# Rest blocks, value weights and key pieces in another order: a two-layer attention kernel on one core

## The chip, the cores and the metric

The kernel runs on one core of a Trainium2 chip. The metric is the device time of one execution in microseconds (us), lower is better. Before the change three runs gave a median of 2765.46 us (2764.1 to 2766.71).

The core's engines work beside each other, each through its own instructions in program order: TensorE (PE, matrix products; PEld are its weight loads), VectorE (DVE), ScalarE (ACT), GpSimd (POOL) and SyncE (SP, which here only issues DMAs).

## The reference

Two attention layers A and B read the same input and are mixed by a gate. Sequence S = 2048, width D = 640, 32 heads of width 20:

```
x = A_x
g = sigmoid((x * gate_w).sum(-1, keepdims=True))
# for z in A, B, with that layer's wqkv and wo:
qkv = (x @ wqkv) split into q, k, v of 32 heads x 20
p   = softmax(q @ k^T * 20 ** -0.5)
o_z = (p @ v) put together to 2048 x 640, @ wo
out = g * o_A + (1 - g) * o_B
```

## The kernel before, in words

**Numbers.** Products of projections run in half precision in two parts: each operand is scaled by a power of two and split into a high and a low part (hi, lo), and three products hi*hi, hi*lo, lo*hi are summed. A projection of 512 positions is thus 15 matmuls (5 slices of the width, three products each). The probabilities and values are multiplied in single precision (line 690).

**Main loop.** Heads are worked in groups of four: 8 groups a layer, 16 in all (numbered from 0, so "the third group" is g = 2 and "the seventh" is g = 6). For each group there are 4 blocks of 512 queries, and for each block 8 steps of two key tiles of 128: 512 steps G (lines 1175 to 1213). One step holds eight score products on TensorE (line 672), each followed by an exponential on ACT (line 675), the value products of the step before (line 690), and eight products for maxima of a later block (line 614), which VectorE reduces (line 625). Softmax maxima are found up to 15 steps ahead. For some heads the maximum over two key chunks a and b is found from the product with the key difference a - b: ACT takes its positive part (line 618), and VectorE adds the product with b and reduces (line 622). The differences of keys are in tiles KD; GpSimd makes them (`key_differences`, lines 494 to 502: five operations), and DMAs spread them into their rows (`spread_differences`).

**Order inside a step.** A step follows one of three handwritten strings STEP (lines 54 to 56): e is a score, m a maximum, V a value product and X a piece of projection work. There is no X in the first string, one in the second, two in the third. Line 1187 picks it: none if no work in the list `fill` may start yet, two if the work is behind its due times, else one. `slot` (line 1125) takes the entry with the earliest due step and runs one of its pieces at each X, until its pieces are used up.

**Pieces.** `project_a` projects the keys and part of the queries of a group, four chunks of 512 positions. APARTS says in how many pieces each chunk of a group is cut, CUTS at which columns (5: 104 or 96 wide; 6: 88 or 80; 4: 128). Every piece is 15 matmuls (line 407) and one move out of the accumulator by ACT (line 434). The keys of g = 2 may start at step 15, due 24 to 36; those of g = 6 at step 136, due 152 to 164. The values' pieces (`project_v`, two for each pair of position tiles) and later the output products stand in the same list.

**Before the main loop** (lines 867 to 1033): input and weights are loaded, scaled and split; x is transposed on TensorE; the keys of group 0 are projected by chunks `a_chunk(0)` to `a_chunk(3)`, each followed by DMAs that spread the rows over the partitions. These DMAs alternate between the SP queue and the POOL queue (`both`, line 945), so a DMA on POOL stands in line with GpSimd's computing. The part of the queries that did not fit beside the keys ("rest") is projected by `r_chunk(0)` to `r_chunk(3)`, one for each block of 512 queries. Then:

- The maxima of the first two query blocks are found (lines 1022 to 1028), two halves for each block. A half has eight units, each of four maxima: two of key differences and two of keys. The first half reads KD[0] (chunks 0 and 1), the second KD[1] (chunks 2 and 3). The heads go in the order (1, 0), so rows 64 to 123 are read first.
- After each unit `go_on` hands TensorE as many matmuls of the series `rest` as that unit's share of the estimate `whole` allows. `rest` holds `r_chunk(1)`, the split of the values' weights (`values_begin`), `r_chunk(2)`, `r_chunk(3)`, the scales for the next group, and all values of the first two groups.
- `split_now` (line 343) splits the values' weights: one copy on ACT (line 344), a scaling (345) and a subtraction (346) on GpSimd, once for 5 x 160 columns and once for the 5 of the gate.

Of the kernel before, what the change touches and what calls it, by code (L numbers as in the profile page):

```python
# [14 lines left out]
OP = mybir.AluOpType  # L15
# [9 lines left out]
NT = S // P  # L25
NC = D // P
# [9 lines left out]
XE = 7  # L36
QKS = 2.0 ** -12
CUTS = {3: (0, 176, 344, 512), 4: (0, 128, 256, 384, 512), 5: (0, 104, 208, 312, 416, 512), 6: (0, 88, 176, 264, 344, 432, 512)}
APARTS = {2: 5, 3: 4, 4: 4, 5: 4, 6: 6}
RPARTS = {1: 4}  # L40
OB = 3
STORED, LOADED = 10, 18
# [19 lines left out]
T_SCORE, T_MODE, T_VALUES, T_READY = 0.217, 0.1, 0.85, 0.39  # L62
# [9 lines left out]
def kernel(  # L72
# [10 lines left out]
    nc = tc.nc  # L83
# [29 lines left out]
    inv_x = consts.tile([P, 1], F32, name="inv_x")  # L113
    inv_g = consts.tile([P, 1], F32, name="inv_g")
# [110 lines left out]
    def set_qk(i, r, inv):  # L225
        nc.vector.tensor_copy(r_qk[i], r)
        e = esc[i]
        nc.vector.tensor_tensor(e, inv[:, 0:1], inv_x, op=OP.mult)
        nc.vector.tensor_scalar(e, e, inv[:, 1:2], float(DH ** -0.5 / QKS ** 2), op0=OP.mult, op1=OP.mult)
        nc.vector.tensor_tensor(e, e, inv_x, op=OP.mult)  # L230

    def set_v(gg, r, inv):
        nc.vector.tensor_copy(r_v[gg], r)

        f = gg % (NG // 2) * 160
        while f < (gg % (NG // 2) + 1) * 160:
            p0 = f % P
            n = min(P - p0, (gg % (NG // 2) + 1) * 160 - f, (P, 32, 64, 32)[p0 // 32])
            nc.vector.tensor_copy(wrow[gg // (NG // 2)][p0:p0 + n, f // P:f // P + 1], inv[p0:p0 + n])
            f += n  # L240
# [102 lines left out]
    def split_now(t, r, hi, lo):  # L343
        nc.scalar.activation(hi, t, AF.Copy, scale=r)
        nc.gpsimd.tensor_scalar(t, t, r, None, op0=OP.mult)
        nc.gpsimd.tensor_tensor(lo, t, hi, op=OP.subtract)
# [7 lines left out]
    def block_tiles(kind):  # L354
        n = 2 if kind == "a" else 1
        return (wts.tile([P, NC, P], F16, name="wbh", tag=f"wh{kind}", bufs=n),
                wts.tile([P, NC, P], F16, name="wbl", tag=f"wl{kind}", bufs=n))
# [58 lines left out]
    def project_chunk(w, hi, lo, ch, parts=None):  # L416

        wh, wl = w
        def pairs(n):
            if now[0] < 0:  # L420
                return ([(wh[:, c, :], b[:, c, n]) for c in range(NC) for b in (xh, xl)]
                        + [(wl[:, c, :], xh[:, c, n]) for c in range(NC)])
            return [(a[:, c, :], b[:, c, n]) for c in range(NC) for a, b in ((wh, xh), (wh, xl), (wl, xh))]

        t0 = ch * QB
        if now[0] >= 0:
            f = work.tile([P, QB], F32, name="fs")
            for k in range(len(parts) - 1):
                if k:
                    yield  # L430
                m = slice(parts[k], parts[k + 1])
                i, pt = take()
                yield from mms(i, pt[:, m], pairs(slice(t0 + m.start, t0 + m.stop)), (m.stop - m.start) / QB)
                nc.scalar.activation(f[:, m], pt[:, m], AF.Copy, scale=QKS)  # L434
                give(i, spend("act", 0.25, clock["done"]))
            nc.gpsimd.tensor_copy(hi, f)  # L436
            nc.gpsimd.tensor_tensor(lo, f, hi, op=OP.subtract)
        else:
            i, pt = take()
            yield from mms(i, pt, pairs(slice(t0, t0 + QB)), 1)  # L440
            give(i, spend("dve", T_MAX, spend("act", T_EXP, clock["done"])))
            nc.scalar.activation(hi, pt, AF.Copy, scale=QKS)
            nc.vector.scalar_tensor_tensor(lo, pt, QKS, hi, op0=OP.mult, op1=OP.subtract)

    def run(gen):
        for _ in gen:
            pass
# [10 lines left out]
    def spread(g, hl, t0, n, q=(0, 1), k=(0, 1), queues=repeat(nc.sync)):  # L458


        cols = slice(t0, t0 + n)
        r0 = 32 * (g % 4)
        qt = QT[g % 2]
        for j in range(2):
            base = 64 * j
            for pair in k:
                f = slice((2 * pair + j) * DH, (2 * pair + j + 1) * DH)
                yield from rows(KT[g % 2][:, pair, cols], base, 0, hl[f], DH, True, queues)
            if 0 in q:
                f = slice(GF + j * DH, GF + (j + 1) * DH)  # L470
                yield from rows(qt[:, 0, cols], base, 0, hl[f], DH, False, queues)
            if 1 in q:
                if j == 0:
                    yield from rows(qt[:, 1, cols], base, 0, hl[GF + 40:P], 8, False, queues)
                f = slice(r0 + 12 * j, r0 + 12 + 20 * j)
                yield from rows(qt[:, 1, cols], base, 8 * (1 - j), rk[g // 4][f, :, cols], 12 + 8 * j, False, queues)
# [6 lines left out]
    def project_r(i, ch):  # L483
        n = slice(ch * QB, (ch + 1) * QB)
        yield from project_chunk(blk["r", i], rk[i][:, 0, n], rk[i][:, 1, n], ch, CUTS[RPARTS.get(i, 3)])
        r_done.add((i, ch))
# [7 lines left out]
    def key_differences(g, hl, f, dd):  # L494

        n = GF
        differences[g] = dd
        nc.gpsimd.tensor_tensor(f[:n], hl[:n, 0, :QB], hl[:n, 0, QB:], op=OP.subtract)
        nc.gpsimd.tensor_tensor(f[:n], f[:n], hl[:n, 1, :QB], op=OP.add)
        nc.gpsimd.tensor_tensor(f[:n], f[:n], hl[:n, 1, QB:], op=OP.subtract)  # L500
        nc.gpsimd.tensor_copy(dd[:n, 0], f[:n])
        nc.gpsimd.tensor_tensor(dd[:n, 1], f[:n], dd[:n, 0], op=OP.subtract)

    def spread_differences(g, queues=repeat(nc.sync), to=None):
        dd = differences.pop(g)
        for j in range(2 if g == 0 else 1):
            for pair in range(2):
                f = slice((2 * pair + j) * DH, (2 * pair + j + 1) * DH)
                yield from rows((KD[g % 2] if to is None else to)[:, pair], 64 * j, 0, dd[f], DH, True, queues)

    def project_a(g, ch):
# [3 lines left out]
        n = slice((ch % 2) * QB, (ch % 2 + 1) * QB)  # L515
        yield from project_chunk(blk["a", g], hl[:, 0, n], hl[:, 1, n], ch, CUTS[APARTS.get(g, 3)])
        if ch == 1:
# [17 lines left out]
    def v_tiles(gg):  # L535
        blk["v", gg] = (wts.tile([P, NC, 161], F16, name="wvh", tag="wvh", bufs=1),
                        wts.tile([P, NC, 161], F16, name="wvl", tag="wvl", bufs=1))
        return blk["v", gg]
# [333 lines left out]
    wv = start.tile([P, NC, 161], F32, name="wv")  # L872
# [50 lines left out]
    hi, lo = blk["a", 0] = block_tiles("a")  # L923
# [8 lines left out]
    hi, lo = blk["r", 0] = block_tiles("r")  # L932
# [23 lines left out]
    def r_chunk(ch, pairs):  # L956
        yield from project_r(0, ch)
        n = slice((ch % 2) * QB, (ch % 2 + 1) * QB)
        run(spread(0, halves[ch // 2][:, :, n], ch * QB, QB, q=pairs, k=(), queues=both))
        spread_done.add((0, ch))  # L960
# [8 lines left out]
    def series(*gens):  # L969
        for gen in gens:  # L970
            yield from gen

    def differences_of(half, to):
        key_differences(0, halves[half], start.tile([P, QB], F32, name="fd"), start.tile([P, 2, QB], F16, name="dd0"))
        run(spread_differences(0, both, to))
# [16 lines left out]
    next(chain)  # L992
    run(chain)
    rv, invv = of_v
    differences_of(1, KD[1])

    def values_begin():
        hi, lo = v_tiles(0)
        split_now(wv[:, :, :160], rv[:, 0:1], hi[:, :, :160], lo[:, :, :160])
        split_now(wv[:, :, 160:161], rv[:, 1:2], hi[:, :, 160:161], lo[:, :, 160:161])  # L1000
        nc.vector.tensor_scalar(inv_g, invv[:, 1:2], inv_x, -1.0, op0=OP.mult, op1=OP.mult)
        yield True

    def next_group():
        set_qk(0, r[:, 0:2], inv[:, 0:2])
        set_v(0, rv[:, 0:1], invv[:, 0:1])
        split_next()
        yield True

    rest = series(r_chunk(1, (0, 1)), values_begin(), r_chunk(2, (0, 1)), r_chunk(3, (0, 1)), next_group(),  # L1010
                  *(project_v(0, j) for j in range(0, NT, 2)))

    halves_done = [0]
    streamed[0] = 0.0
    whole = (3 * 3 * NC + NT * 3 * NC * 0.33) * T_SCORE

    def go_on(share):

# [36 lines left out]
    for g in range(2 * NG):  # L1055
        b = g * step
        n = g + 1
        if n < 2 * NG:
            parts = APARTS.get(n, 3)
            fill += [((-8, 15)[g] if g < 2 else b + AFROM, b + ADUE + ADUES * ch if g else 4 + 3 * ch, parts, project_a(n, ch))  # L1060
# [188 lines left out]
```

## Time and profile before

| What | Value |
|---|---|
| Median of three runs | 2765.46 us |
| The profiled execution | 2765.39 us, span 2763.6 us |
| PE | 2725.5 us, 99% of the span |
| ACT | 2525.4 us, 91% |
| DVE | 2441.0 us, 88% |
| POOL | 671.5 us, 24% |
| DMA | 125.60 MB, mean 45 GB/s |

The profile is of one execution. A row of a timeline gives start, duration (both us), engine, line, operation, tiles (out<-in), shapes and count; in square brackets stands how long the engine was idle before, and what ended it. A row of the chain of work gives start, duration, and what was on the chain. A row of a table by stage gives the stretch, its length, then for each engine its busy time and, in brackets, its instructions; then the granted TensorE clock (1.00 is full), the DMA share and GB/s. Where such a table is restricted to one line of the code, it counts only that line's instructions. Matmuls are pipelined, so their durations overlap; starts are better read than durations.

### The profile page before, as it was taken

Reading aid. Unit: us, or ns where it says so; the run is one execution under the profiler, and the core shown is the slowest. Engines: PE = TensorE matmul, PEld = TensorE weight load, DVE = VectorE, ACT = ScalarE, POOL = GpSimd, SP = SyncE. Lnnn points to the kernel's source line nnn. Section 1 sums busy time; section 2 is a strip of 40 time slices with the busy share of each in tenths; the row PEclk is TensorE's granted clock in tenths of the full one; section 3 lists DMA queues with packets and bytes.
Section 4 is the critical chain, followed back from the end, with each engine's and each line's share of the span. In section 5 each row is a group of like instructions: output and inputs, shape, how many; then the busy total and the mean of one; then the engine's idle time right before and its main releaser. Section 6 shows DMA issues by size and latency. Waiting matters only on the chain.

```text
span 2763.6 us, 62604 instructions
## 1 busy us (share of the span) xinstructions
PE 2725.5 (99%) x23453; PEld 938.0 (34%) x23453; DVE 2441.0 (88%) x4780; ACT 2525.4 (91%) x5140; POOL 671.5 (24%) x914
## 2 busy tenths in 40 slices
PE   7999999999999999999999999999999999999998
PEld 3433333333333332333333333333333333333222
DVE  7789999999999889888888998989988898999982
ACT  4999999999999999999999899999999999999997
POOL 6322223222123422311222111222342202100111
PEclk8999999999999999999999999999999999999999
DMA  4021102010120212102012230221201112122112
GB/s 142 17 57 26 31 11 47 8 31 16 25 55 20 60 35 56 41 9 61 20 41 66 60 84 26 60 56 48 65 16 42 30 50 63 32 77 64 47 47 76
DMA packets 176433, 125.60 MB, mean 45 GB/s; under 512 B 105216, under 2 KB 145976, under 8 KB 176128
## 3 DMA queue, kind: packets, MB, share of 16 engines
q1 hardware_dynamic: 173584, 119.99, 17.0%
q8 instruction: 183, 3.00, 0.5%
q0 software_dynamic: 1600, 0.96, 0.2%
q14 instruction: 122, 1.00, 0.1%
q10 hardware_dynamic: 944, 0.66, 0.1%
HBM read 55.53 MB, written 31.86 MB: 32 GB/s over the span
## 4 chain that ended last, share of the span: by engine, by line
PE 93%; DVE 4%; ACT 1%; DMA 1%; issue 0%; POOL 0%; SPq 0%; POOLq 0%; DVEq 0%; ACTq 0%
PE acc L690 35%; PE bank L407 20%; PE bank L614 20%; PE bank L672 18%; DVE mpart L625 2%; ACT pt L675 1%; DMA ws<-in_A_wqkv_dram 0%; DVE rl L622 0%; PE bank L854 0%; DVE ot L777 0%; DMA xs<-in_A_x_dram 0%; PE bank L900 0%; ACT rl L618 0%; DVE wmax L258 0%; DMA kd<-dd 0%
## 5 line engine op out<-in xcount | busy, mean ns | idle before, releaser
L675 ACT ACTIVATE pt<-bank 128x512 f32<-128x512 f32 x4096 | 2173.2, 615 | 147.9 <-PE bank L672 105.3
L625 DVE TENSOR_REDUCE mpart<-bank 128x1 f32<-128x512 f32 x2944 | 1842.4, 681 | 220.7 <-PE bank L614 117.4
L690 PE MATMUL acc<-pt,v 128*21 128x512 f32 x8192 | 1081.7, 600 | 0.7 <-DVE ot L777 0.6
L672 PE MATMUL bank<-qt,kt 64*128 64x512 f16 x4096 | 1039.1, 380 | 4.7 <-DVE mpart L625 2.7
L614 PE MATMUL bank<-kt,qt 60*128 60x512 f16 x3520 | 1010.6, 381 | 3.6 <-DVE mpart L625 1.0
L614 PEld LDWEIGHTS <-qt 60*128 60x128 f16 x4096 | 237.9, 94 | 906.8 <-issue 846.1
L622 DVE CUSTOM_DVE_ANT_0 rl<-bank,rl 128x512 f32<-128x512 f32 x576 | 386.7, 677 | 13.3 <-ACT rl L618 8.6
L618 ACT ACTIVATE rl<-bank 128x512 f32<-128x512 f32 x576 | 339.6, 600 | 11.9 <-PE bank L614 11.3
L407 PE MATMUL bank<-xx,wbh 128*128 128x168 f16 (+7 forms) x2600 | 291.4, 234 | 1.5 <-DVE wbh L926 1.0
L672 PEld LDWEIGHTS <-kt 64*128 64x128 f16 x4096 | 229.2, 94 | 178.8 <-issue 69.9
L690 PEld LDWEIGHTS acc<-pt,v 128*21 128x21 f32 x8192 | 143.0, 99 | 426.2 <-issue 421.9
L407 PE MATMUL bank<-xx,wbl 128*128 128x168 f16 (+7 forms) x1300 | 259.9, 232 | 0.0
L785 POOL TENSOR_TENSOR ot<-ot,sq 128x512 f32<-128x512 f32 x63 | 66.0, 1047 | 736.7 <-DVE sq L782 718.1
L407 PEld LDWEIGHTS <-wbh 128*128 128x128 f16 x2600 | 196.5, 98 | 118.4 <-issue 112.7
L614 PE MATMUL bank<-kd,qt 60*128 60x512 f16 x576 | 204.3, 380 | 2.3 <-DMA kd<-dd 2.2
L436 POOL CAST cq<-fs 128x512 f16<-128x512 f32 x60 | 36.6, 610 | 500.8 <-ACT fs L434 500.8
L407 PE MATMUL bank<-woh,o_in 128*128 128x320 f16 (+3 forms) x700 | 157.7, 290 | 0.0
L407 PE MATMUL bank<-wvh,xx 128*128 128x160 f16 (+1 forms) x1280 | 156.0, 234 | 0.0
L407 PEld LDWEIGHTS <-xx 128*128 128x128 f16 x1920 | 131.3, 97 | 56.1 <-issue 53.8
L407 PE MATMUL bank<-wvl,xx 128*128 128x160 f16 (+1 forms) x640 | 137.6, 232 | 0.0
L407 PEld LDWEIGHTS <-wbl 128*128 128x128 f16 x1300 | 127.4, 98 | 4.4 <-issue 1.3
L407 PEld LDWEIGHTS <-o_in 128*128 128x128 f16 (+1 forms) x1050 | 87.3, 97 | 90.7 <-issue 68.5
(140 smaller groups left out, 1251.8 us busy)
## 6 DMA issues: line engine op xcount, KB each, us to landing
y_scr<-y_out SPq DMA_DIRECT2D x48, 320.0 KB
y_out<-y_scr SPq DMA_DIRECT2D x32, 320.0 KB
kt<-cq SPq DMA_DIRECT2D x120, 80.0 KB
o_scr<-on SPq DMA_DIRECT2D x240, 40.0 KB
o_in<-o_scr SPq DMA_DIRECT2D x64, 96.0 KB
kt<-cq SPq DMA_DIRECT2D x136, 40.0 KB
wstage<-in_B_wqkv_dram SPq DMA_DIRECT2D x13, 400.0 KB
xs<-in_A_x_dram SPq DMA_DIRECT2D x8, 640.0 KB
```

What stands on the lines that cost most here:

```text
L407: nc.tensor.matmul(out_ap, a, b, start=(k == 0), stop=(k == len(pairs) - 1))
L436: nc.gpsimd.tensor_copy(hi, f)
L614: nc.tensor.matmul(pt, QT[g % 2][r, pair, q0:q0 + P], k, start=True, stop=True)
L618: nc.scalar.activation(relus[u, j], pt, AF.Relu)
L622: nc.vector.tensor_tensor_reduce(rl, pt, rl, 1.0, LOW, OP.add, OP.max, m)
L625: nc.vector.tensor_reduce(m, pt, axis=AX.X, op=OP.max)
L672: nc.tensor.matmul(et, KT[g % 2][r, pair, kt * P:(kt + 1) * P], QT[g % 2][r, pair, qb * QB:(qb + 1) * QB], start=True, stop=True)
L675: nc.scalar.activation(pt, et, AF.Exp, scale=factor(g // 4))
L690: nc.tensor.matmul(acc[32 * h:32 * h + VW, :], V[(g // 2) % 2][:, kt, (g % 2) * GH + h, :], ptiles.pop((G, kk, h)), start=(kt == 0), stop= ...
L785: nc.gpsimd.tensor_tensor(t3, t3, sq.unsqueeze(2).to_broadcast([P, 16, 32]), op=OP.mult)
```

## The change

Three things move. The values' weights are split right after their scales are known, ahead of the second key differences (KD[1]); before, this stood in `rest` behind `r_chunk(1)`. `r_chunk(1)` runs ahead of the first maxima, and is no longer in `rest`; `whole` is reduced by its share. And the keys of g = 2 and g = 6 are cut into four pieces a chunk instead of five and six.

```diff
-APARTS = {2: 5, 3: 4, 4: 4, 5: 4, 6: 6}
+APARTS = {2: 4, 3: 4, 4: 4, 5: 4, 6: 4}
...
     run(chain)
     rv, invv = of_v
+    hi, lo = v_tiles(0)
+    split_now(wv[:, :, :160], rv[:, 0:1], hi[:, :, :160], lo[:, :, :160])
+    split_now(wv[:, :, 160:161], rv[:, 1:2], hi[:, :, 160:161], lo[:, :, 160:161])
+    nc.vector.tensor_scalar(inv_g, invv[:, 1:2], inv_x, -1.0, op0=OP.mult, op1=OP.mult)
     differences_of(1, KD[1])
-
-    def values_begin():
-        hi, lo = v_tiles(0)
-        split_now(wv[:, :, :160], rv[:, 0:1], hi[:, :, :160], lo[:, :, :160])
-        split_now(wv[:, :, 160:161], rv[:, 1:2], hi[:, :, 160:161], lo[:, :, 160:161])
-        nc.vector.tensor_scalar(inv_g, invv[:, 1:2], inv_x, -1.0, op0=OP.mult, op1=OP.mult)
-        yield True
+    run(r_chunk(1, (0, 1)))
...
-    rest = series(r_chunk(1, (0, 1)), values_begin(), r_chunk(2, (0, 1)), r_chunk(3, (0, 1)), next_group(),
+    rest = series(r_chunk(2, (0, 1)), r_chunk(3, (0, 1)), next_group(),
                   *(project_v(0, j) for j in range(0, NT, 2)))
...
-    whole = (3 * 3 * NC + NT * 3 * NC * 0.33) * T_SCORE
+    whole = (2 * 3 * NC + NT * 3 * NC * 0.33) * T_SCORE
```

## The prediction

> **What bounds the kernel now.** I read the page's chain of work that ended last, then the same chain cut to the first 160 us, then engine timelines there, and last a table by stage for the main loop.
>
> ```profile
> span 2763.6 us, 62604 instructions
> ...
> PE 93%; DVE 4%; ACT 1%; DMA 1%; issue 0%; POOL 0%; SPq 0%; POOLq 0%; DVEq 0%; ACTq 0%
> PE acc L690 35%; PE bank L407 20%; PE bank L614 20%; PE bank L672 18%; DVE mpart L625 2%; ACT pt L675 1%; DMA ws<-in_A_wqkv_dram 0%; DVE rl L622 0%; PE bank L854 0%; DVE ot L777 0%; DMA xs<-in_A_x_dram 0%; PE bank L900 0%; ACT rl L618 0%; DVE wmax L258 0%; DMA kd<-dd 0%
> ```
>
> TensorE carries 93% of the chain. So an edit counts if it removes TensorE work or TensorE idle time, or if a step becomes so short that another engine ends it.
>
> Two stages change. The first is the stage before the main loop, up to the first scores (line 672):
>
> ```profile
> 49.45 2.27 DMA kd<-dd
> 51.86 0.71 PE bank L614 x4
> ...
> 67.81 0.54 PE bank L614 x4
> 68.35 0.97 PE bank L407 x4
> ...
> 72.93 0.95 PE bank L407 x12
> ...
> 104.86 0.58 PE bank L672 x4
> ```
>
> At 51.86 the first maxima wait for a DMA of key differences. Afterwards TensorE alternates between four maxima (a "quartet", 0.54) and a piece of the "rest" (0.97 for four 512-wide matmuls, 0.95 for twelve of the values' 161-wide ones, switching included). The stage ends at 104.86.
>
> The second is the main loop: 512 steps of eight exponentials on ACT. A step has room for one piece X of projection work. Below, each window starts and ends at a step's first exponential, found by counting eight L675 instructions a step. The first table counts them; the second gives every engine (PE, PEld, DVE, ACT, POOL).
>
> ```profile
> 188.01:288.32 100.31, 86.55 (x161) 1.00 0.10 21
> 793.78:913.83 120.05, 104.61 (x192) 1.00 0.13 32
> 303.82:343.65 39.83, 33.98 (x65) 1.00 0.09 20
> 425.33:434.74 9.41, 8.16 (x16) 1.00 0.05 10
> ```
>
> ```profile
> 188.01:288.32 100.31, 100.02 (x944) 32.91 (x941) 95.00 (x192) 94.61 (x204) 23.57 (x35) 1.00 0.10 21
> 793.78:913.83 120.05, 119.22 (x1130) 37.73 (x1129) 114.36 (x224) 111.97 (x241) 41.79 (x46) 1.00 0.13 32
> 303.82:343.65 39.83, 39.83 (x378) 14.03 (x376) 36.57 (x69) 38.18 (x81) 5.46 (x9) 1.00 0.09 20
> 425.33:434.74 9.41, 9.23 (x68) 2.12 (x70) 9.13 (x19) 8.91 (x19) 6.67 (x6) 1.00 0.05 10
> ```
>
> From the top: the third group's keys in fifths, 20 steps, 100.31/20 = 5.02 a step; the seventh group's in sixths, 24 steps, 5.00 a step; keys in quarters, 8 steps, 4.98 a step; two steps with no X, 4.71 each. (A stray exponential at a window's edge makes 161 and 65.) In the third row TensorE has no gap. In the fourth VectorE is busy 9.13 of 9.41: without X it is VectorE that nearly ends the step.
>
> **Edit 1: rest block 1 and the values' split move ahead.** TensorE and GpSimd are in-order queues here, so I follow both.
>
> ```profile
> 42.60 2.32 PE L407 MATMUL bank<-xx,wbh 128*128 128x512 f16 x10
> 44.76 0.59 PE L407 MATMUL bank<-xx,wbl 128*128 128x512 f16 x2
> ...
> 49.32 0.38 PE L195 MATMUL bank<-dg,ones 2*128 2x4 f32 x2
> 51.86 0.50 PE L614 MATMUL bank<-kd,qt 60*128 60x512 f16 x2 [2.16 <-DMA kd<-dd]
> ...
> 66.38 0.39 PE L614 MATMUL bank<-kd,qt 60*128 60x512 f16 x2
> ```
>
> ```profile
> 47.76 1.99 POOL L455 DMA_DIRECT2D kd<-dd  x4
> ...
> 55.25 1.17 POOL L498 TENSOR_TENSOR fd<-cq 80x512 f32<-80x512 f16 x1
> ...
> 60.74 1.99 POOL L455 DMA_DIRECT2D kd<-dd  x4
> ...
> 65.27 2.30 POOL L345 TENSOR_SCALAR wv<-wv,both 128x800 f32<-128x800 f32 x1
> ...
> 69.96 1.06 POOL L455 DMA_DIRECT2D qt<-cq  x2
> ```
>
> *What it fills.* Ten matmuls start 42.60 to 44.76, 0.216 each. Block 1 is 15 of them, 3.24 us. Its operands are there at 49.70, where the scales' product (L195) ends, so it fills the idle 2.16 us and puts the first maxima at 52.94 instead of 51.86. Four maxima plus the switch to and fro are 0.54 + 0.97 - 4 x 0.216 = 0.65.
>
> *What it delays.* GpSimd is in unbroken work from 47.76 to 69.96: DMA issues, second differences (55.25 to 60.74, 5.49), issues of KD[1] and of block 1's queries, then the values' split (65.27 to 69.96, 4.69). The change puts the split first. It starts at 55.25, the differences at 59.94, and they end at 65.43. Behind them, in the POOL and SP queues alike, stand KD[1]'s DMAs and block 1's query rows. KD[0] needed 51.86 - 47.76 = 4.10 from the end of its differences to the matmul that reads it (j = 1 is read first, issued third on SP). So KD[1] can be read at 65.43 + 4.10 = **69.53**.
>
> *Who waits.* The first matmul on KD[1] is the first of the second half of block 0, the ninth quartet, at 66.38 before. `go_on` hands out rest by shares of `whole`: after 8 of 32 quartets a quarter, (45 + 79.2)/4 = 31.05 before, so 32 matmuls; (30 + 79.2)/4 = 27.3 now, so 28. Hence TensorE would come to it at 52.94 + 28 x 0.216 + 8 x 0.65 = 64.2. It waits about 5.3 us, and everything behind it in TensorE's queue waits too. The idle time is not removed; it moves and grows.
>
> *What comes back.* At the ninth quartet 15 + 28 = 43 rest matmuls of 512 are done, against 32 before: 11 x 0.216 = 2.38 fewer to do.
>
> ```profile
> 49.70:51.86 2.16, 0.00 (x1) 0.03 (x1) 0.76 (x2) 0.33 (x1) 2.16 (x6) 1.00 0.39 88
> 51.86:55.87 4.01, 4.01 (x14) 1.04 (x15) 1.58 (x5) 1.99 (x4) 4.00 (x8) 0.57 0.37 87
> 66.38:104.86 38.48, 38.46 (x367) 22.19 (x368) 34.38 (x113) 32.85 (x83) 13.95 (x23) 1.00 0.08 18
> ```
>
> From the ninth quartet to the end took 38.48; now 36.10. VectorE's 34.38 at the 97% that the no-X row shows would need 35.4, so it does not bind yet. The middle row shows the price of an idle TensorE: after the 2.16 us gap the granted clock was 0.57 over 4.01 us, 4.01 x 0.43 = 1.7 lost. A gap of 5.3 should cost as much, up to twice that if two such stretches follow. Sum: 69.53 + 36.10 + 1.7 = 107.3, that is **+2.5 us**. Bounds: +0.8 without the clock loss; +6.6 with two cold stretches (1.7 more) and nothing given back (2.4 more).
>
> The Trainium skill, page "TensorE: Matmul & The Clock Gate", Part 1, has the clock fall to half after an idle window of about 3.4 us and stay there until a busy one has passed. By it the 2.16 us gap should have cost nothing, which the 0.57 row contradicts; the new gap of 5.3 us would cost one window, an estimated 1.7, so by rule and by row the sum is +2.5.
>
> ```profile
> 59.93 1.16 ACT L344 ACTIVATE wvh<-wv,both 128x800 f16<-128x800 f32 x2
> ```
>
> The other pieces cost nothing. ACT's share of the split (1.16) moves from between the maxima to about 51, where ACT was busy 0.33 of 2.16; the small scale on VectorE likewise. Block 1's query rows, queued behind KD[1] on SP and POOL, are first read at the seventeenth quartet, eight quartets with their rest after 69.53, some 11 us. Without that cover each would delay its first reader by its own length.
>
> **Edit 2: quarters instead of fifths and sixths.**
>
> ```profile
> 226.93 0.27 PE L407 MATMUL bank<-xx,wbh 128*128 128x104 f16 x2
> ...
> 227.72 0.39 PE L672 MATMUL bank<-qt,kt 64*128 64x512 f16 x1
> ```
>
> ```profile
> 423.98 0.29 PE L407 MATMUL bank<-xx,wbh 128*128 128x128 f16 x2
> ...
> 424.92 0.39 PE L672 MATMUL bank<-qt,kt 64*128 64x512 f16 x1
> ```
>
> A fifth (104 columns) occupies TensorE 0.79, a quarter 0.94. Four fewer pieces for group 3, eight fewer for group 7. One piece is taken a step, the earliest due first. Group 3's keys now end at step 31, not 35; all behind moves up four steps, the next work may start at 66, so 60 to 63 go empty and join the existing pair 64 and 65 (the no-X row). Group 7's end at 151, not 159; the values' pieces fill up to 161, group 8's keys may start at 168, so 162 to 167 go empty, and two more slots some steps later, when output products have moved up.
>
> Group 3: 20 steps, 100.31, become 16 x 4.98 + 4 x 4.71 = 98.5: -1.8. Group 7: 24 steps, 120.05, become 16 x 4.98 + 8 x 4.71 = 117.4: -2.7. Against this, the first step with X after a run without it is late:
>
> ```profile
> 434.74:440.31 5.57, 4.29 (x9) 1.00 0.00 0
> 440.31:445.50 5.19, 4.25 (x8) 1.00 0.05 6
> ```
>
> 5.57 against 5.19, 0.4 for each new run; group 7 makes about two, 0.8. Sum -3.7. That is one end. The other end is the best step in narrow pieces:
>
> ```profile
> 238.57:243.40 4.83, 4.25 (x9) 1.00 0.02 0
> 793.78:798.62 4.84, 4.21 (x9) 1.00 0.26 72
> ```
>
> If the excess of 5.02 over 4.83 is VectorE's other work of those steps (95.00/20 = 4.75 busy a step, against 4.57 in quarters) and remains, a quarter saves nothing: 16 x 4.98 + 4 x 4.71 - 20 x 4.83 = +1.9 and 117.4 - 24 x 4.84 = +1.2, at worst +3.9 with the runs' cost. Where X is narrow that VectorE work is visible; under a quarter's 4.98 it should be covered, so I stand near the first end: **-2.5 us**.
>
> **Sum.** +2.5 - 2.5 = 0. The profiled execution took 2765.39 (span 2763.6, 1.8 around it), the median is 2765.46: the forecast is 2765.5.
>
> **The rivals.** A measurement of this kernel can tell about 0.2% (5.5 us) from no change.
>
> *KD[1] is not waited for.* If the ninth quartet finds its operand, the stage is 52.94 + 32 x 0.65 + 30 x 0.216 + 240 matmuls of the values at (0.95 - 0.10)/12, 17.0; with the 3.1 of scattered waits that 38.48 holds over its own pure work (24 x 0.65 + 13 x 0.216 + 17.0 = 35.4), it ends near 100.3, -4.6. With -2.5: 2758.4. For it: the filled gap at 51.86 is real. Against it: GpSimd has no gap from 47.76 to 69.96 in which the split could hide. If block 1 were not started at 49.70 (the change not doing what it says) the wait would only be shorter.
>
> *The wait is not made up.* One mechanism, at the ninth quartet: TensorE resumes cold and the other engines, which lost the 3.15 us from 66.38 to 69.53, then end the stage. Start +4.9 to +6.6; with the quarters anywhere from -2.5 to 0 that is 2768 to 2772, say 2769.5. It decides from where the start loses more than the quarters give. For it: VectorE needs 34.38 of 38.48 already. Against it: 35.4 is below 36.10.
>
> *The quarters give nothing*, the second end above, the start as forecast: 2765.5 + 2.5 to + 6.4, say 2769.
>
> **Chances.** Forecast 0.55 (own range 2762 to 2768.5); no wait 0.10; not made up 0.22; quarters useless 0.13. No wait is faster by over 0.2% about two times in three, with a little from the forecast's tail: 0.08. Past 2771 lie about a third of the two slow rivals and a little of the forecast's tail: 0.14. Within 0.2%: 0.78. The range leaves out most of the first rival and the worst third of the slow ones: 2760 to 2771.
>
> **What would show it.** In the changed profile the idle 2.16 before the first maxima is gone and they start near 53; the values' scaling on POOL (L345's operation) stands at 55; a wait of about 5 on "DMA kd<-dd" ends near 69.5, with a low granted clock behind it; the first scores come near 107. The 128-wide pieces of groups 3 and 7 run at 4.98 a step, and steps 60 to 65 without X at about 4.7. I am wrong if the ninth quartet starts before 66, if the first scores are before 104, or if the no-X steps take 4.98.

## The result, and the profile after

The changed kernel took 2768.62 us (median of 22 runs, 2768.01 to 2769.76), the kernel before, in turn with it on the same chip, 2765.37 (22 runs, 2763.44 to 2767.71). The ratio is 1.0013, 95% interval 1.0007 to 1.0018: slower by 0.13%, 3.25 us. The forecast was 2765.5; the time is within the 0.2% that the prediction took as no change, and in the stated range of 2760 to 2771, but 3.1 us above the middle and 0.1 above the 2762 to 2768.5 that the forecast had for itself. Of all runs told here one, of e3, was slow (6399.79 us); the ratios leave it out. The profiled execution took 2768.17, 2.78 more than the one of before.

The page of the changed kernel, its span, busy times and chain by engine:

```profile
span 2766.4 us, 62244 instructions
...
PE 2724.8 (98%) x23273; PEld 939.3 (34%) x23273; DVE 2441.7 (88%) x4780; ACT 2528.6 (91%) x5128; POOL 671.6 (24%) x914
...
PE 93%; DVE 4%; POOL 1%; ACT 1%; DMA 1%; issue 0%; SPq 0%; POOLq 0%; DVEq 0%; ACTq 0%
```

TensorE was busy 0.7 us less (2725.5 before), yet the span is 2.8 longer. New in the chain is GpSimd, with 1%. Where it enters is seen in TensorE's timeline at the start (start, duration, then the idle time before in brackets):

```profile
49.33 0.38 PE L195 MATMUL bank<-dg,ones 2*128 2x4 f32 x2
49.64 2.33 PE L407 MATMUL bank<-xx,wbh 128*128 128x512 f16 x10
...
52.99 0.39 PE L614 MATMUL bank<-kd,qt 60*128 60x512 f16 x2
...
63.57 0.81 PE L407 MATMUL bank<-xx,wbl 128*128 128x512 f16 x3
69.72 0.71 PE L614 MATMUL bank<-kd,qt 60*128 60x512 f16 x2 [5.34 <-DMA kd<-dd]
```

The idle 2.16 us before the first maxima is filled: block 1 follows the scales' product at once, and the maxima start at 52.99. But the ninth quartet starts at 69.72 after an idle 5.34 us, and what ended the idle time is the DMA of key differences. The chain of work of the same kernel, cut to this stretch, tells what these waited for:

```profile
55.36 2.30 POOL wv L345
...
57.74 1.71 POOL wvl L346
...
60.06 1.10 POOL fd L498
...
64.36 1.17 POOL dd L502
...
65.55 0.76 SPq L453
...
66.35 0.76 SPq L453
...
67.16 2.42 DMA kd<-dd
...
69.72 1.13 PE bank L614 x4
```

Read downwards, GpSimd's queue has the values' split (L345, L346) and then the second differences (L498 to L502); behind them stand their issue on SP, the transfer and the quartet. The table by stage shows the wait and its price (length, then PE, PEld, DVE, ACT, POOL, the granted clock, DMA share, GB/s):

```profile
65.94:69.35 3.41, 0.00 (x0) 0.00 (x0) 0.00 (x0) 0.00 (x0) 3.41 (x8) 1.00 0.30 69
69.35:72.77 3.42, 3.05 (x13) 1.11 (x13) 1.59 (x5) 1.68 (x3) 3.42 (x8) 0.50 0.32 71
72.77:76.18 3.41, 3.41 (x33) 1.97 (x32) 3.34 (x15) 3.02 (x8) 3.38 (x6) 1.00 0.33 76
```

For 3.41 us no engine but GpSimd is busy, with issues of DMAs; for the next 3.42 TensorE has the clock 0.50, then 1.00 again. The first scores come at 107.49 (104.80 before).

For the main loop the same table, windows laid from step to step by counting exponentials, steps numbered from 0: first steps 15 to 31 of the changed kernel (the third group's sixteen quarters, steps 15 to 30), then four plain ones of these, one late one (step 25), and the six steps without X (59 to 64):

```profile
185.79:266.82 81.03, 80.66 (x754) 28.31 (x751) 74.65 (x153) 77.47 (x164) 17.88 (x25) 1.00 0.13 30
246.93:266.82 19.89, 19.89 (x190) 6.95 (x187) 18.42 (x41) 19.10 (x41) 3.53 (x4) 1.00 0.27 59
236.36:242.02 5.66, 5.39 (x51) 1.84 (x48) 5.53 (x11) 4.79 (x10) 1.10 (x2) 1.00 0.01 3
409.47:438.23 28.76, 27.77 (x198) 6.41 (x196) 27.86 (x59) 27.18 (x54) 8.50 (x8) 1.00 0.16 37
```

A plain quarter step takes 19.89/4 = 4.97, all of it TensorE, but the 16 steps take 81.03/16 = 5.06, because some are late (5.66 in the third row). A step without X takes 28.76/6 = 4.79. The same four steps of the kernel before, in fifths, and the step behind them, a late one:

```profile
243.40:262.94 19.54, 19.54 (x189) 6.46 (x187) 18.37 (x41) 18.64 (x41) 3.54 (x4) 1.00 0.28 60
262.94:268.34 5.40, 5.36 (x49) 1.72 (x48) 5.32 (x11) 4.72 (x13) 0.00 (x0) 1.00 0.00 0
```

A plain fifth step takes 4.885. Where the pieces end is seen in TensorE's timeline. The first projection matmuls behind the third group's keys are 160 wide, a values' piece; they stand in step 31 of the changed kernel (from 266.82) and in step 35 of the kernel before (from 283.00):

```profile
270.91 0.24 PE L407 MATMUL bank<-wvh,xx 128*128 128x160 f16 x1
```

```profile
286.69 0.24 PE L407 MATMUL bank<-wvh,xx 128*128 128x160 f16 x1
```

So the fifths take steps 15 to 34, from 183.09 to 283.00, and the prediction's window begins one step late: 188.01:288.32 runs from step 16 to step 36, without the first fifth (4.92) and with a values' piece (5.33).

Over the whole loop, stages laid from step to step, in us against the kernel before (e1 and e2 are the change's two parts, e6 has only the seventh group in quarters; e10 and e12 move weight maxima in quarters and in fifths; all told below):

| Steps | before | after | e1 | e2 | e6 | e10 | e12 |
|---|---|---|---|---|---|---|---|
| start to first exponential | 105.54 | +2.69 | +3.72 | +0.20 | +0.71 | +0.24 | +0.06 |
| 0 to 15 | 77.55 | +0.01 | +0.02 | +0.01 | +0.01 | -0.15 | -0.15 |
| 15 to 35 | 99.91 | +2.53 | +0.01 | +2.53 | 0.00 | +1.13 | -1.37 |
| 35 to 67 | 162.51 | -1.75 | 0.00 | -1.76 | -0.02 | +1.24 | +2.11 |
| 67 to 135 | 343.40 | +0.05 | +0.01 | 0.00 | -0.01 | 0.00 | 0.00 |
| 135 to 176 | 208.73 | +0.44 | +0.16 | +0.45 | +1.33 | +0.43 | +1.28 |
| 176 to 200 | 127.41 | +1.02 | +0.02 | +1.01 | +1.01 | +1.02 | -0.01 |
| 200 to 300 | 527.86 | -0.51 | +0.33 | -0.51 | -0.51 | -0.29 | -0.01 |
| 300 to 309 | 49.82 | -2.57 | -0.09 | -2.57 | -2.57 | -2.57 | 0.00 |
| 309 to 511 | 1038.58 | +0.12 | +0.27 | +0.30 | +0.50 | +1.14 | -0.01 |
| loop, 0 to 511 | 2635.76 | -0.65 | +0.74 | -0.54 | -0.26 | +1.96 | +1.84 |
| from step 511 to the end | 22.26 | +0.78 | +0.24 | -0.28 | +0.94 | +0.56 | +0.49 |

So the profiled execution's +2.8 is +2.69 at the start, -0.65 in the loop and +0.78 at the end. Small sums over the loop are to be read with care: e1, e3, e4, e7 and e8, whose loop has the code of before, took 0.43 to 0.83 longer in it than the kernel before.

### The profile page after: what moved, and what is told of

Same layout as the page of the kernel before. It is cut to its first block, busy times and chain, and to the rows that moved or that the text cites. A ratio compares the mean times of both kernels' runs of the same rounds, so it can differ in the third digit from the quotient of the medians.

```text
span 2766.4 us, 62244 instructions
## 1 busy us (share of the span) xinstructions
PE 2724.8 (98%) x23273; PEld 939.3 (34%) x23273; DVE 2441.7 (88%) x4780; ACT 2528.6 (91%) x5128; POOL 671.6 (24%) x914
## 4 chain that ended last, share of the span: by engine, by line
PE 93%; DVE 4%; POOL 1%; ACT 1%; DMA 1%; issue 0%; SPq 0%; POOLq 0%; DVEq 0%; ACTq 0%
PE acc L690 35%; PE bank L407 20%; PE bank L614 20%; PE bank L672 18%; DVE mpart L625 2%; ACT pt L675 1%; DMA ws<-in_A_wqkv_dram 0%; PE bank L854 0%; DVE rl L622 0%; DMA xs<-in_A_x_dram 0%; DVE ot L777 0%; PE bank L900 0%; POOL kt L455 0%; POOL wv L345 0%; DMA kd<-dd 0%
## 5 line engine op out<-in xcount | busy, mean ns | idle before, releaser
L672 PE MATMUL bank<-qt,kt 64*128 64x512 f16 x4096 | 1042.3, 380 | 4.2 <-DVE mpart L625 2.3
L672 PEld LDWEIGHTS <-kt 64*128 64x128 f16 x4096 | 231.2, 95 | 199.0 <-issue 88.5
L407 PE MATMUL bank<-xx,wbh 128*128 128x168 f16 (+3 forms) x2480 | 287.4, 236 | 1.4 <-DVE wbh L926 1.0
L407 PE MATMUL bank<-xx,wbl 128*128 128x168 f16 (+3 forms) x1240 | 257.9, 235 | 0.0
L407 PEld LDWEIGHTS <-wbh 128*128 128x128 f16 x2480 | 192.7, 98 | 111.0 <-issue 104.7
L407 PE MATMUL bank<-woh,o_in 128*128 128x320 f16 (+3 forms) x700 | 157.8, 290 | 0.0
L407 PE MATMUL bank<-wvh,xx 128*128 128x160 f16 (+1 forms) x1280 | 156.9, 234 | 0.0
L407 PEld LDWEIGHTS <-xx 128*128 128x128 f16 x1920 | 131.3, 97 | 58.8 <-issue 56.2
L407 PE MATMUL bank<-wvl,xx 128*128 128x160 f16 (+1 forms) x640 | 137.8, 232 | 0.0
L407 PEld LDWEIGHTS <-wbl 128*128 128x128 f16 x1240 | 121.0, 98 | 4.7 <-issue 1.3
L407 PEld LDWEIGHTS <-o_in 128*128 128x128 f16 (+1 forms) x1050 | 87.4, 97 | 90.6 <-issue 67.4
```

The lines of the kernel that those rows point to most:

```text
L407: nc.tensor.matmul(out_ap, a, b, start=(k == 0), stop=(k == len(pairs) - 1))
L672: nc.tensor.matmul(et, KT[g % 2][r, pair, kt * P:(kt + 1) * P], QT[g % 2][r, pair, qb * QB:(qb + 1) * QB], start=True, stop=True)
```

## The experiments

The theory: GpSimd's in-order queue has no room between 47.76 and 69.96, so whatever of the split and the second differences stands behind is late, and TensorE pays for the idle time a second time in the clock; the quarters save little. The rivals were that block 1's place at the front is the cause, and, for the quarters, that their VectorE work is covered so that they give their full 2.5. Each kernel had five rounds against the kernel before on its chip. Starts are compared as the time from the scales' product (L195) to the first scores (L672): 55.48 before, 58.16 after. The scales' product itself, which no edit touches, stood at 49.08 to 49.69 in the traces whose first stretch at clock 0.50 lasts 13.65 us, and at 49.96 to 50.68 where it lasts 17.07 (e4, e6, e7, e8, e9).

### e1_start_only: the first part alone

```diff
+    split_now(...)          # both splits and inv_g, out of rest
     differences_of(1, KD[1])
+    run(r_chunk(1, (0, 1)))
```

> Only the first edit (values' split ahead of the second key differences, rest block 1 ahead of the first maxima); pieces in fifths and sixths as before. Theory W (the wait for KD[1] at the ninth quartet makes the whole difference, the quarters about nothing): the first scores come 2.7 later, 2765.4 + 2.7 = 2768.1, the whole of the change's +3.25 within 1. Rival Q (the quarters are worth -2.5 as forecast and the stage before the loop cost more elsewhere): 2771.

Measured: 2770.09 against 2766.08, ratio 1.0015 (1.0006 to 1.0024). Start 59.44, +3.96. TensorE's timeline, then the table by stage:

```profile
69.49 0.70 PE L614 MATMUL bank<-kd,qt 60*128 60x512 f16 x2 [5.35 <-DMA kd<-dd]
```

```profile
68.96:72.37 3.41, 2.88 (x13) 1.10 (x13) 1.43 (x5) 1.68 (x3) 3.41 (x8) 0.50 0.31 66
72.37:75.79 3.42, 3.42 (x22) 1.81 (x19) 2.64 (x13) 1.88 (x4) 3.39 (x6) 0.50 0.33 78
```

The wait is the changed kernel's to 0.01 us, but two stretches ran at 0.50 instead of one: 3.41 x 0.5 = 1.7 more lost, of which 1.28 shows (59.44 - 58.16). The first part costs, and it costs at the start; the loop, with the code of before, is longer by 0.74. By its time alone, +4.0, the run lies between the theory's +2.7 and rival Q's +5.6; the trace decides for the theory, with a second cold stretch which the theory did not have.

### e2_quarters_only: the second part alone

```diff
-APARTS = {2: 5, 3: 4, 4: 4, 5: 4, 6: 6}
+APARTS = {2: 4, 3: 4, 4: 4, 5: 4, 6: 4}
```

> Only the second edit (quarters for groups 3 and 7). Theory W: within 1 of before, 2764.5 to 2766.5; in the profile the sixteen 128-wide steps of group 3 take 5.06 and not 4.98, since VectorE's other work there is not covered. Rival Q: 2762.9, -2.5.

Measured: 2765.17 against 2766.08, ratio 0.9994 (0.9985 to 1.0003). By the interval alone, -4.1 to +0.8 us, the forecast -2.5 isn't excluded. The stages are sharper: down to step 309 the loop's stages equal those of the changed kernel within 0.05 us, and the loop is 0.54 shorter in all. +4.0 from e1 and -0.9 from here make +3.1; measured together +3.25. The two intervals are about 2.5 us wide on either side, so this sum shows little by itself; the equal stages show that the quarters do the same with and without the first part. The expectation's 5.06 for a quarter step came out (81.03/16).

### e3_block1_first: block 1 ahead, the split left in the rest

```diff
     differences_of(1, KD[1])
+    run(r_chunk(1, (0, 1)))
...
-    rest = series(r_chunk(1, (0, 1)), values_begin(), ...
+    rest = series(values_begin(), ...
```

> Rest block 1 ahead of the first maxima, the values' split left behind it in the rest; fifths and sixths. Theory W, with GpSimd's queue as the limit: KD[1] can be read at 60.74 + 4.10 = 64.84, so the ninth quartet waits only 0.6; but now the values' split ends near 69.4 and the first values' matmul comes to it near 65.9 and waits 3.5. First scores 104.5 to 106.2, time 2765 to 2767. Rival M (block 1 ahead of the maxima is bad by itself, as the first maxima start 1.1 later and nothing is won back): first maxima at 53 and no long wait behind, first scores near 106, 2766.5.

Measured: 2769.01 against 2766.08, ratio 1.0010 (1.0000 to 1.0019). Start 58.62, +3.14. Timeline and table:

```profile
70.38 0.29 PE L407 MATMUL bank<-wvl,xx 128*128 128x161 f16 x1 [3.80 <-POOL wvl L346]
```

```profile
66.15:69.56 3.41, 0.43 (x3) 0.18 (x2) 3.38 (x7) 1.00 (x2) 3.33 (x2) 1.00 0.20 43
69.56:72.97 3.41, 2.59 (x16) 1.45 (x15) 1.68 (x9) 1.09 (x2) 3.33 (x9) 0.50 0.21 49
72.97:76.38 3.41, 3.41 (x21) 1.47 (x18) 1.67 (x6) 1.56 (x5) 3.38 (x6) 0.50 0.32 71
```

The wait for the key differences is gone, and the split's low part is late instead: TensorE, 15 matmuls further, reaches the values before GpSimd has split their weights. With the differences first, it is the split that ends last. The expectation had this wait (3.5), but not the two cold stretches behind it (3.4 us lost), and so 2765 to 2767.

### e4_split_first: the split ahead, block 1 left in the rest

```diff
+    split_now(...)          # both splits and inv_g, out of rest
     differences_of(1, KD[1])
...
-    rest = series(r_chunk(1, (0, 1)), values_begin(), r_chunk(2, ...
+    rest = series(r_chunk(1, (0, 1)), r_chunk(2, ...
```

> The values' split ahead of the second key differences, rest block 1 left among the maxima as before; fifths and sixths. Theory W: KD[1] readable near 69.5, the ninth quartet comes near 66.4 and waits 3.1, then TensorE is cold for a stretch (1.7): 2765.4 + 3.1 + 1.7 = 2770.2. Rival M: the split is harmless, 2765.4.

Measured: 2771.41 against 2766.08, ratio 1.0019 (1.0010 to 1.0028). Start 60.45, +4.97. TensorE's timeline:

```profile
52.47 0.50 PE L614 MATMUL bank<-kd,qt 60*128 60x512 f16 x2 [1.56 <-DMA kd<-dd]
...
70.19 0.71 PE L614 MATMUL bank<-kd,qt 60*128 60x512 f16 x2 [4.98 <-DMA kd<-dd]
```

Both waits stand here, the old one in front and the new one. So it is the split's place alone that makes the wait near 70; block 1's place only fills the gap in front. The wait is 4.98 and not the 3.1 expected: the 1.56 in front was followed by no cold stretch, and TensorE reached the ninth quartet 14.68 us after the scales' product instead of 17.06. Behind the wait the clock is 0.50 for 6.83 us, two stretches where one was expected.

### e7_split_behind: block 1 ahead, the split right behind the second differences

```diff
     differences_of(1, KD[1])
+    split_now(...)          # both splits and inv_g, out of rest
+    run(r_chunk(1, (0, 1)))
```

> Rest block 1 ahead of the first maxima; the values' split ahead of them too, but behind the second key differences instead of ahead; fifths and sixths. Theory G (GpSimd's queue can give KD[1] or the split values by 65, not both; the later one is waited for, and a wait over about 3 us costs one or two cold stretches of TensorE's clock of 1.7 each): KD[1] readable at 64.8, the split values at 66.8, about 1 us of wait, no cold clock, first scores near 102, 2765.5 - 3 = 2762.5. Rival M (block 1 ahead of the maxima is bad by itself): like the run with the split left in the rest, 2768.5.

Measured: 2764.43 against 2765.48, ratio 0.9996 (0.9987 to 1.0005). Start 53.22, -2.26. The longest wait in TensorE's timeline from the maxima to the scores:

```profile
68.30 0.23 PE L407 MATMUL bank<-wvl,xx 128*128 128x161 f16 x1 [1.45 <-POOL wvl L346]
```

The split now stands ahead of block 1's query transfers in GpSimd's queue, so the wait shrinks from e3's 3.80 to 1.45, and the clock stays at 1.00. The same parts in another order turn +2.7 into -2.3 at the start. The median gains only 1.05; in the profiled execution the scales' product came 1.03 later than before, and the loop took 0.70 longer.

### e8_split_on_vector: the first part, the split's low part on VectorE

```diff
-        nc.gpsimd.tensor_scalar(t, t, r, None, op0=OP.mult)
-        nc.gpsimd.tensor_tensor(lo, t, hi, op=OP.subtract)
+        nc.vector.scalar_tensor_tensor(lo, t, r, hi, op0=OP.mult, op1=OP.subtract)
```

> The first edit, but the low part of the values' weights is one operation on VectorE (weight x scale - high part) in place of two on GpSimd; fifths and sixths. Theory G: GpSimd is free for the second differences at 55.25, KD[1] readable at 64.8, the ninth quartet comes to it near 64.3, wait under 1, no cold clock; first scores near 101, 2765.5 - 3.9 = 2761.6. Rival M: 2766.5 or more.

Measured: 2763.93 against 2765.48, ratio 0.9995 (0.9986 to 1.0004). Start 52.26, -3.22. (Line numbers are one lower here and in e11.)

```profile
70.10 0.23 PE L406 MATMUL bank<-wvh,xx 128*128 128x161 f16 x1 [0.60 <-DVE mpart L621]
```

With 4.69 us taken off GpSimd's queue neither the differences nor the split are waited for; the longest wait left, 0.60, is for VectorE. That shows the cause directly: the order of e1, without the work on GpSimd, loses nothing. The median gains only 1.55; in the profiled execution the scales' product came 1.35 later than before, and the loop took 0.50 longer.

### e6_group7_quarters: the seventh group alone

```diff
-APARTS = {2: 5, 3: 4, 4: 4, 5: 4, 6: 6}
+APARTS = {2: 5, 3: 4, 4: 4, 5: 4, 6: 4}
```

> Quarters for group 7 alone, all else as before. Theory S (each piece change is a sum over steps: group 3 +0.8; group 7 +1.5 by step 200 and -3.0 later, between steps 256 and 400, where the output products that moved up meet other waits): 2765.5 - 1.5 = 2764.0. Rival Q (the forecast: group 7 -1.7 within its own steps): the steps 135 to 200 get shorter by 1.7, not longer.

Measured: 2766.27 against 2765.48, ratio 1.0000 (0.9991 to 1.0009); the expected 1.5 did not come. In the table above: +1.33 in steps 135 to 176, where the expectation's rival had -1.7 down to step 200, then +1.01 and -3.08 behind. Of the 0.9 by which e6's +1.33 exceeds e2's +0.45, 0.85 stands in step 148 alone (5.76 against 4.91). That step took 5.10 before, and 5.54 in e4 and 6.40 in e12, which both have sixths there. As e4's loop has the code of before, at least 0.4 of such a difference is spread between executions. The one large gain of the quarters, steps 300 to 309, comes with this group. Table by stage for L407 alone, the kernel before and then the changed one, where the length is the same as here:

```profile
1652.90:1702.72 49.82, 13.75 (x162) 11.39 (x162) 1.00 0.15 42
```

```profile
1657.38:1704.63 47.25, 11.66 (x132) 9.29 (x132) 1.00 0.16 44
```

These nine steps hold 30 matmuls fewer, two pieces: before, steps 301 and 308 ran two pieces each, now one. Counted step by step, the changed kernel's twelve pieces fewer are missing in steps 59 to 62 (group 3), 161 to 166, 301 and 308 (group 7). The gain is real, but it stands over 130 steps behind the place where it was booked.

### e9_quarters_short_maxima: quarters, short weight maxima

The weight maxima (line 258) run in VectorE's queue, among others during steps 12 to 25 and 136 to 146. Here they read 8 columns of 160, and a pair takes 0.17 and 0.16 us instead of 0.64 and 0.48.

```diff
-                    largest(m[:, k, 2 * i:2 * i + 1], st["t"][:, 0:3])
+                    largest(m[:, k, 2 * i:2 * i + 1], st["t"][:, 0:3, 0:8])
```

> Quarters for groups 3 and 7, the start as before, and VectorE's weight maxima inside the main loop (line 286 and 291) over 8 of 160 columns; this leaves out most of that search, so the scales come from a part of the weights. Theory D (VectorE's extra work in the steps of groups 3 and 7 is what makes their quarters 5.06 a step instead of 4.98): steps 15 to 31 take 79.7 instead of 81.0, steps 135 to 151 about 79.9 instead of 81.2; 2762.5 in all. Rival B (the excess is the change of query blocks and of groups): unchanged, 2765.

Measured: 2762.82 against 2765.48, ratio 0.9990 (0.9981 to 0.9999). The time is near the expected 2762.5, but not by the expected way: the 16 quarters of group 3 took 80.84 (81.03 in e2), not 79.7, and steps 15 to 35 stayed at +2.33 (e2 +2.53). That fells the theory that the length of these reductions makes the steps late. The loop is 2.93 shorter than before; 2.57 of it are steps 300 to 309, as in e2. The step at 234.00 in the table by stage, and TensorE's timeline in it:

```profile
234.00:239.66 5.66, 5.39 (x51) 1.84 (x48) 4.83 (x10) 4.79 (x11) 0.34 (x2) 1.00 0.01 3
```

```profile
234.65 0.37 PE L614 MATMUL bank<-kt,qt 60*128 60x512 f16 x1 [0.27 <-ACT pt L675]
```

VectorE has only 4.83 of 5.66 to do, and the step is as late as with full maxima (5.66). Of the 0.64 above e10's 5.02 for this step (next section), 0.27 is TensorE's wait for an exponential; the rest is TensorE's own work, 5.39 with two matmuls more in the step.

### e10 and e12: the same maxima 32 steps later, in quarters and in fifths

```diff
-QKMAX = (0, 10, 42, 10)
+QKMAX = (0, 42, 42, 10)
```

e10 has this beside e2's quarters, e12 alone.

> Quarters for groups 3 and 7, the start as before, and VectorE's eight weight maxima of layer A (with the planner's account of them) moved from steps 10 to 26 to steps 42 to 58. Theory D (those tasks, with the banks that the planner then chooses, make the late steps 18, 26 and 32): steps 15 to 31 take 79.7 instead of 81.0, and steps 39 to 59 grow by about as much; all in all 2765. Rival B (ends of query blocks and the change of group make them): steps 15 to 31 stay at 81.0, steps 39 to 59 too.

> Fifths and sixths and the start as before, with the same eight maxima moved to steps 42 to 58. Theory D: the 20 steps in fifths fall from 99.9 to about 97.4, and about 1.3 comes back in steps 39 to 59; 2764.3. Rival B: steps 15 to 35 stay at 99.9; 2765.5.

Measured: e10 2767.84 against 2765.72, ratio 1.0008 (0.9999 to 1.0017); e12 2766.02, ratio 1.0003 (0.9994 to 1.0012), each above what was expected (2765 and 2764.3). The table by stage of e2, for steps 25 and 49, and then e10 for the same steps:

```profile
233.87:239.53 5.66, 5.39 (x51) 1.84 (x48) 5.53 (x11) 4.79 (x11) 1.10 (x2) 1.00 0.02 3
356.24:361.26 5.02, 5.02 (x49) 1.70 (x47) 4.75 (x10) 4.77 (x12) 0.41 (x2) 1.00 0.01 3
```

```profile
233.41:238.43 5.02, 5.02 (x49) 1.77 (x47) 4.75 (x10) 4.77 (x12) 0.41 (x2) 1.00 0.01 3
354.84:360.50 5.66, 5.39 (x51) 1.84 (x48) 5.53 (x11) 4.79 (x11) 1.10 (x2) 1.00 0.01 3
```

The late step goes where the maxima go: 5.66 and 5.02 change places. In fifths the step behind the third group's last plain ones, 5.40 before, becomes (e12, table by stage):

```profile
261.95:266.84 4.89, 4.89 (x49) 1.62 (x47) 4.39 (x8) 4.69 (x13) 0.00 (x0) 1.00 0.00 0
```

In steps 15 to 35 the move takes 1.37 off in fifths (99.91 to 98.54) and 1.40 off in quarters (e2's 102.44 to 101.04). So the maxima's price is the same under a quarter as under a fifth: the wider piece covers none of it. The expectation had more, 2.5 in fifths, so part of the late steps' excess is not the maxima's. It is not won either, since steps 35 to 67 lose 2.1 in e12 and 3.0 in e10 against e2; of e12's 2.1, 1.39 stands in step 63, for which no run shows a cause.

### e11_after_split_on_vector: the whole change with the split's low part on VectorE

The changed kernel with e8's edit.

> The changed kernel (both edits) with the low part of the values' weights as one operation on VectorE in place of two on GpSimd. Sum of what the single runs showed, each against the scales' product L195: stage before the loop -3.2, loop -0.5: 2765.5 - 3.7 = 2761.8; if the first stage's gain is as small as its own run's median had it (-1.5): 2763.5.

Measured: 2762.87 against 2765.72, ratio 0.9989 (0.9980 to 0.9998). It is faster than the kernel before by 0.11%, while the changed kernel is slower than that by 0.13%. Start 52.21, -3.27; loop 2635.00, 0.1 below the changed kernel's. Timeline, and the table by stage for the stretch in which the changed kernel stood still:

```profile
52.22 1.20 DVE L345 SCALAR_TENSOR_TENSOR wvl<-wv,both,wvh 128x800 f16<-128x800 f32 x2 [1.03 <-ACT wvh L344]
...
69.06 0.23 PE L406 MATMUL bank<-wvh,xx 128*128 128x161 f16 x1 [0.60 <-DVE mpart L621]
```

```profile
64.00:69.70 5.70, 5.10 (x41) 2.61 (x39) 5.51 (x23) 4.68 (x11) 5.70 (x13) 1.00 0.33 74
```

The changed kernel for the same window:

```profile
64.00:69.70 5.70, 0.38 (x2) 0.01 (x1) 1.25 (x6) 0.29 (x1) 5.62 (x11) 0.97 0.22 49
```

1.20 us on VectorE, idle for 1.03 ahead of them, take the place of 4.69 on GpSimd, and TensorE does 5.10 us of work where it did 0.38. VectorE is now the busy one beside it (5.51 of 5.70).

## Why the prediction was right at the start and wrong in the loop

The time fell into the range, but the mechanism was right in one half only: the start came as forecast and the quarters did not. Nearest to what happened is the third rival, to which the prediction gave 0.13.

- **The gap is filled and moved: right.** First maxima 52.94 forecast, 52.99 measured; split on GpSimd 55.25, 55.36; ninth quartet reached 64.2, 64.38 (69.72 - 5.34); KD[1] readable 69.53, 69.72; wait 5.3, 5.34. Following two in-order queues by hand was enough for 0.2 us.
- **The clock: right in the profiled execution, and partly luck.** One cold stretch of 3.42 at 0.50 costs 1.7, as forecast; e1 with the same wait had two, the "up to twice that" of the prediction. The Trainium skill, page "TensorE: Matmul & The Clock Gate", Part 1, calls the window free-running, and the runs agree: behind these waits the stretches are 3.41 or twice that, and they don't begin at the wait's end. The prediction read the page's rule as one idle time of some length; what counts is how a fixed grid of 3.41 cuts it.
- **What comes back: right.** From the ninth quartet to the first scores 107.49 - 69.72 = 37.77, less 1.7 of clock 36.1; forecast 36.10. Start +2.5 forecast, +2.69 measured.
- **The cover of edit 1's other pieces: right.** No wait for block 1's query rows or ACT's copy shows in TensorE's timeline from 50 to the first scores.
- **The quarters, -2.5: wrong; the term was -0.65** (-0.54 in e2; against e1, and in e11 against e8, which share their starts, -1.39 and -1.26). The step that failed is "under a quarter's 4.98 it should be covered", with the sum that hung on it, "16 x 4.98 + 4 x 4.71 = 98.5: -1.8". The 5.02 of a fifth's step was a mean of plain ones and late ones. Plain ones take 4.885, so 20 of them 97.7; 16 plain quarters and four steps without X take 16 x 4.97 + 4 x 4.79 = 98.7. Without any late step the quarters thus lose 1.0. The maxima's part of the late steps was not covered: moving it away takes 1.40 off the quarters (e10) and 1.37 off the fifths (e12). Measured for the third group, steps 15 to 67: 2.53 - 1.75 = +0.78, where the forecast had -1.8.
- **Its sums began from windows one step late.** The 20 fifths took 99.91 (5.00 a step) and not 100.31, the 24 sixths 119.66 (788.90 to 908.56) and not 120.05. With these the prediction's own terms are -1.4 and -2.3 instead of -1.8 and -2.7. Its empty steps 60 to 65 are 59 to 64 in the numbering used here.
- **The seventh group came near its sum, and that is luck.** Down to step 309 it gave +0.44 + 1.02 - 0.51 - 2.57 = -1.62, where the forecast had -1.9. But its own steps, 135 to 176, did not get shorter, and the two last of its eight freed slots, booked at 5.00 - 4.71 = 0.3 each, came in steps 301 and 308, where a step with two pieces became one with one: 2.09 us of L407's time less (13.75 to 11.66), of the 2.57. The prediction named the move of the pieces behind and priced nothing but the empty slots.
- **The sizes.** 128-wide steps: 4.98 forecast; 4.97 plain, 5.06 as a mean. Steps without X: 4.71 forecast from two steps, 4.79 over six.
- **The end: not foreseen, +0.78.** Eight matmuls (L829) at the very end, in TensorE's timeline of the kernel before and then of the changed one:

```profile
2750.02 1.12 PE L829 MATMUL bank<-rt,fs 16*128 16x128 f32 x8 [0.45 <-ACT rt L825]
```

```profile
2752.05 1.88 PE L829 MATMUL bank<-rt,fs 16*128 16x128 f32 x8 [0.45 <-ACT rt L825]
```

Both have the same wait ahead of them. The table by stage, again of the kernel before and then of the changed one, has the clock:

```profile
2748.98:2752.40 3.42, 1.81 (x11) 1.16 (x11) 1.14 (x5) 1.04 (x5) 0.39 (x2) 1.00 0.00 0
2752.40:2755.81 3.41, 3.35 (x14) 1.93 (x14) 1.10 (x2) 1.08 (x3) 2.05 (x5) 0.50 0.00 0
```

```profile
2748.81:2752.23 3.42, 2.55 (x20) 1.68 (x17) 0.81 (x2) 0.86 (x2) 0.00 (x0) 1.00 0.00 0
2752.23:2755.65 3.42, 2.58 (x12) 1.80 (x12) 0.88 (x4) 0.91 (x4) 0.85 (x3) 0.50 0.00 0
2755.65:2759.06 3.41, 3.41 (x15) 1.92 (x14) 1.16 (x3) 1.05 (x2) 1.85 (x4) 0.50 0.04 17
```

Before, the clock fell 2.38 us behind these matmuls' start, and for one stretch; in the changed kernel 0.18 behind it, and for two. All thirteen traces have the same code at the end. The six with two stretches there (the changed kernel, e1, e6, e10, e11, e12) end 0.24 to 0.94 later than before; the six others with one stretch (e2, e3, e4, e7, e8, e9) 0.41 earlier to equal. So I put the +0.78 down to where the clock's stretches fall, not to the change.

**The rivals.** *KD[1] is not waited for* fell, but e8 and e11 show that state made on purpose: the start is then 3.2 to 3.3 better, where this rival had 4.6. *The wait is not made up* came near in time (2769.5) and not in mechanism: no wait for VectorE shows in TensorE's timeline of that stage; e1 came to +3.96 by the clock's second stretch. *The quarters give nothing* (2769) is the nearest to what happened, in place and in time (2768.62).

**What stays open.** Why the late steps go with the maxima though not with their length. In e9 the order of the instructions on TensorE, ScalarE and VectorE was e2's throughout, and the wait (0.27 on an exponential) the same: the kernel counts each such reduction as 0.5 when it is written out (line 260), whatever it reads. Between e2 and e10 TensorE's order by line and tile differs in 2 places, ScalarE's in none. What is left is VectorE's order, or which accumulator bank each product gets, which the trace doesn't name; neither was tried by itself. Nor is it shown what makes step 148 vary.

## What to carry to other kernels

An idle gap filled on one engine is a gain only if the queues that feed the next wait are not lengthened by the same edit: follow each of them instruction by instruction, and move the work to an engine that has the room (here 4.69 us on GpSimd became 1.20 on an idle VectorE). And a mean step time isn't the price of a step: check that the window holds the pieces that it is said to hold, split it into plain and late steps before multiplying, and price the freed slot by what a step without that work takes, here 4.79 against 4.885.

## What the runs showed of the hardware that was not expected

- The granted clock changed only on a grid of 3.41 us: in all thirteen traces the stretches at 0.50 last 3.41, 6.83, 13.65 or 17.07, but for the last one, which the trace's end cuts. Before the main loop it fell to 0.50 after a window with TensorE busy 0.00 (changed kernel), 0.43 (e3), 1.25 (before) and 1.45 us (e9). The kernel before in the table by stage:

```profile
49.05:52.46 3.41, 1.25 (x8) 0.51 (x6) 0.76 (x2) 0.79 (x2) 3.41 (x8) 1.00 0.40 90
52.46:55.87 3.41, 3.41 (x11) 0.84 (x11) 1.58 (x5) 1.80 (x4) 3.40 (x7) 0.50 0.37 85
```

- So an idle 2.16 us was enough for a cold stretch, since most of one window held it, while 1.56 us in e4 and 1.45 in e7 brought none (TensorE busy 2.40 and 2.11 in the window), and neither did the first 1.56 of the changed kernel's wait (62.53 to 65.94, busy 1.85). The "over about 3 us" of e7's expectation was too long. At the end of the kernel it fell after 1.81 and 2.55 us as well (rows above), so the busy time that the profile counts is not the whole measure; what else counts is not shown.
- A cold window had to be nearly full of work before the main loop to end the state: after 3.05 (changed kernel) and 3.41 us busy it did, after 2.88 (e1) and 2.59 (e3) another one followed. At the end of the kernel less was enough: 2.64 (e4) and 2.89 (e7) ended it, 2.58 (changed kernel) did not. Hence the same wait of 5.34 and 5.35 us cost one stretch in one execution and two in the other, 1.7 us apart, with 0.17 us between them of TensorE's time in the window (3.05 against 2.88).
